# Weight and x splits of an attention kernel moved to GpSimd, and its last numerator groups put in other PSUM banks

## The chip, the cores and the metric

The kernel runs on one core of one Trainium2 chip. The metric is device time in microseconds for one execution, and less is better. A profiled execution gives besides it a span (first to last instruction) and a trace of every engine.

## What is computed

The reference is FAVOR attention followed by two feed-forward layers, all in float32:

```
q_s, k_s = q * scale, k * scale            # q, k, v: (4, 8, 576, 64), omega: (128, 64)
phi(x):  h = x @ omega.T - |x|^2 / 2;  h -= max(h);  exp(h) / sqrt(128)
kv  = phi(k_s).T @ v;   z = sum over tokens of phi(k_s)
x   = (phi(q_s) @ kv) / (phi(q_s) @ z + 1e-6)
h   = x @ w_in;  x = silu(h) @ w_out                       # 2304 x 512, d_ff 2048
out = (silu(x @ w_gate) * (x @ w_val)) @ w_out2            # d_ff 1536
```

## The kernel before, in words

**Three parts in a row.** First attention (to about 136.8 us of the trace), then the up and down products of the first layer, then those of the second. The feed-forward products use Strassen's scheme: seven block products for eight, on sums of blocks. Each operand goes as two parts, `hi` (a copy rounded to a short float32 form, `F32R`) and `lo` (the rest, original minus `hi`), and three matmuls stand for one (hi*hi, hi*lo, lo*hi).

**Attention.** Eight units (two batches of one pair of heads each, 1152 tokens) of nine chunks of 128 tokens, worked on in pairs of chunks: 36 iterations of `two_steps(d)` (L881), and a few more at the end. An iteration issues, for each engine in its own order: on TensorE `proj` of the next pair (L730, 32 matmuls), `kv` of the pair before (L772), perhaps the numerators of one group of three chunks (`num`, L818, 24 matmuls), the four transposes of `q_turn` (L794), and perhaps the transposes back of a group (`turn`, L850). On VectorE two maxima (`soft`, L752), and for a group `divide` (L838: add, reciprocal, multiply) and `take_out` (L856, copy from PSUM). On ScalarE eight exponentials (L754) and the copy `qp` (L800). `proj` has two sets of two PSUM banks (0 to 3); banks 5 to 7 go round among `kv` sums and groups of numerators in the queue `px` (L666).

**Work put between.** Attention leaves TensorE's operands of the next part to be made. `early` (L504) holds two queues: `conv` (three jobs of `w_in`, one of `w_out`) and `x` (the first of three blocks of the attention's own result). At the end of each iteration `feed` (L508) takes from each queue, for each of two steps and each engine, at most the given number of operations, in order, if their inputs were issued at least some steps ago (`made`) and their space was given back two steps ago (`given`). So the order is settled when the program is built, and on the chip each engine works through its list, waiting on semaphores. A conversion job (`conv_job`, L315) decodes the weights, which arrive in 64-bit words, in two halves: `first` on ScalarE (L343), `shift` (L350) and `low` (L357) on VectorE; then four Strassen sums on GpSimd (L376); then, in four parts of 256, 512, 512 and 512 columns, `hi` (L406 on VectorE, L408 on ScalarE) and `lo` (L419, VectorE). The decoded halves lie in three slots (`f_c`), which the last `lo` of a job gives back, and the next jobs' `first` takes them. `x_prep` (L534) makes seven operands of two parts of 384 columns each: `hi` on ScalarE (L571), `lo` on VectorE (L580), and eight differences (L601), here on GpSimd.

**The end of attention.** Unit 7's three groups of numerators are left over. `last_nums` (L989) issues them after the first Strassen product of the up part (L1060), into banks 7, 6 and 5, with their divides; then `mark(5, 6)` (L1034) writes banks 5 and 6. `last_turn` (L1005) turns each group between later products. In the up part a planner with costs (`Op`, `flush`) sets the order of everything else; the store of hidden values (L1086) and the loads of later x blocks (L553) share the one queue of SyncE (SP).

Of the kernel before, what the change touches and what calls it, by code (L numbers as in the profile page):

```python
# [9 lines left out]
F32 = mybir.dt.float32  # L10
# [32 lines left out]
def kernel(  # L43
# [270 lines left out]

    def conv_job(kind, i, dram=None):  # L315
        b = {}
# [84 lines left out]
        def hi(k):  # L401
            def go():
                if ("w", 0) not in b:
                    b["w", 0], b["w", 1] = f_w.take(), f_w.take()
                if k in (1, 2):
                    nc.vector.tensor_copy(dst(0, k), src(k))  # L406
                else:
                    nc.scalar.activation(dst(0, k), src(k), AF.Copy)  # L408

            n = 256 * (parts[k][1] - parts[k][0])  # L410
            eng, c = ("DVE", cost("COPY", n)) if k in (1, 2) else ("ACT", cost("ACT", n))
            return Op(
                eng, c, go, ins=[key(*x) for x in after[k]], outs=[key("hi", k)],
                slots=lambda: None if ("w", 0) in b else (f_w, 2),
            )

        def lo(k):
            def go():
                nc.vector.tensor_sub(dst(1, k), src(k), dst(0, k).bitcast(F32))  # L419
                if k == 3:  # L420
                    done(clk["end"])
                    W[kind, i] = (b["w", 0], b["w", 1])

            n = 256 * (parts[k][1] - parts[k][0])
            outs = [key("lo", k)] + ([("W", kind, i)] if k == 3 else [])
            return Op("DVE", cost("DVE", n), go, ins=[key("hi", k)], outs=outs)

# [80 lines left out]
    def feed(name, s, limits):  # L508


        for e, n in limits.items():
            q = early[name]
            for _ in range(n):
                o = next((o for o in q if o.eng == e), None)
                if o is None or o.ready() is None:
                    break
                if any(k in made and s - made[k][0] < made[k][1] for k in o.ins):
                    break
                slots = o.slots() if callable(o.slots) else o.slots
                if slots is not None and any(s - given.get(id(x), -9) < 2 for x, _ in list(slots[0].q)[: slots[1]]):  # L520
                    break
                q.remove(o)
                now[0] = s
                o.emit()
                for k in o.outs:
                    made[k] = (s, {"SP": 5 if name == "x" else 3, "POOL": 2}.get(e, 1))
        while urgent:
            urgent.pop(0).emit()
# [5 lines left out]
    def x_prep(m, s, raws, temps, eng, early=False, before=None, after=(), then=None):  # L534
# [31 lines left out]
        def hi(name, of, j, after):  # L566
            def go():
                if (m, s, name) not in X:
                    X[m, s, name] = tuple(f_op.take() for _ in range(2))
                o = cut(X[m, s, name][0], j * N, N)  # L570
                nc.scalar.activation(o, (b[of, j] if (of, j) in b else r[of, j]).bitcast(F32), AF.Copy)  # L571

            return Op(
                "ACT", cost("ACT", N), go, ins=[after], outs=[key("hi", name, j)], slots=(f_op, 2) if j == 0 else None
            )

        def lo(name, of, j):
            def go():
                h, l = (cut(x, j * N, N) for x in X[m, s, name])
                nc.vector.tensor_sub(l, (b[of, j] if (of, j) in b else r[of, j]).bitcast(F32), h.bitcast(F32))  # L580
                if name == "T4" and temps:
# [7 lines left out]
            if name == "T4":  # L589
                outs.append(key("end", j))  # L590
            return Op("DVE", cost("DVE", N), go, ins=[key("hi", name, j)], outs=outs)

# [275 lines left out]
    def store(u):  # L868
        B, p = u_of(u, 0)
        for b in range(UB):  # L870
            T["xd", B, p + b] = 0.0
            made["xd", B, p + b] = (step_of[0], 3)
        nc.sync.dma_start(
            out=x_d[B][p : p + UB].rearrange("b p s -> p b s"), in_=xts.pop(u).rearrange("p (b s) -> p b s", b=UB)
        )

    groups, to_divide, to_turn, to_take = [], [], [], []

    early["conv"].extend(chain(conv_job("in", 0), conv_job("in", 1), down_job(0, 0), conv_job("in", 2)))
    early["x"].extend(x_prep(0, 0, xr1, False, "POOL", early=True))  # L880
    def two_steps(d):  # L881
# [28 lines left out]
        coming = sum((u, b) not in kvps and LEFT[u, b] == NCH // 2 + 1 for u, b in {x[:2] for y in kv_parts(d) for x in y}) if 0 <= d < ND else 0  # L910
        if groups and groups[0][2] < d and len(px) and len(px) - 1 + len(turns) + len(ended) >= coming and not (groups[0][:2] != (NU - 1, 0) and groups[0][0] == NU - 1) and d < ND:
            u, g, _ = groups.pop(0)
# [15 lines left out]
        if d < ND:  # L928
# [8 lines left out]
            for s in (2 * d, 2 * d + 1):  # L937
                step_of[0] = s
                if s >= 8:
                    feed("conv", s, {"SP": 1, "ACT": 1, "DVE": 1, "POOL": 1})  # L940
                if s >= 27:
                    feed("x", s, {"SP": 4, "ACT": 2, "DVE": 2, "POOL": 1})

# [45 lines left out]
    def last_nums():  # L989

        for (u, g, _), b in zip(left_over, (7, 6, 5)):
            num(u, g, b)
# [643 lines left out]
```

## Time and profile before

| | before |
|---|---|
| median of 3 runs | 916.19 us (915.04 to 919.54) |
| the profiled execution's own time | 919.76 us |
| its span | 917.6 us |
| TensorE busy, share of the span | 883.3 us, 96% |
| VectorE | 641.3 us, 70% |
| ScalarE | 558.0 us, 61% |
| GpSimd | 120.8 us, 13% |

Engines: PE is TensorE's matmuls, PEld its weight loads, DVE is VectorE, ACT ScalarE, POOL GpSimd, SP SyncE. The ends of matmuls are modelled, so a busy PE is not one at its peak; the pace of PE is better read from the starts of the same step in successive iterations. The shares of the whole span say little about attention, which is a seventh of it.

### The profile page before, as it was taken

The numbers are of one execution on the slowest core, as the hardware profiler recorded it, in microseconds if no ns is written. First come the engines' busy times: TensorE is split into PE (matmuls) and PEld (weight loads), VectorE is DVE, ScalarE is ACT, GpSimd is POOL, SyncE is SP. The second block draws the span as 40 slices with busy tenths as digits, with TensorE's granted clock in tenths as the row PEclk, the third lists the DMA queues.
The fourth block names the chain that finished last, engine by engine and source line by source line (L and its number), as shares of the span: only waits on it lengthen the run. The fifth ranks groups of instructions, "written<-read, shape, count | busy, mean of one in ns | idle before, by whom it ended". The sixth has DMA issues, their size and how long they took to land.

```text
span 917.6 us, 18106 instructions
## 1 busy us (share of the span) xinstructions
PE 883.3 (96%) x6887; PEld 856.2 (93%) x6887; DVE 641.3 (70%) x1048; ACT 558.0 (61%) x1186; POOL 120.8 (13%) x152
## 2 busy tenths in 40 slices
PE   8988899999999998999999999999999999999998
PEld 7777689899999988999998999999999998999997
DVE  3897877665664497686789898574646547959683
ACT  5988787666667774444457775554545357445553
POOL 0112300214344000000000024130303100000000
PEclk9999999999999999999999999999999999999999
DMA  6676507858989984707604746362625168371702
GB/s 208 225 232 213 175 29 253 260 176 287 299 277 366 373 325 120 225 1 216 197 23 157 231 148 215 112 224 70 230 75 188 64 219 297 102 237 53 240 1 70
DMA packets 105864, 170.08 MB, mean 185 GB/s; under 512 B 8752, under 2 KB 87984, under 8 KB 105776
## 3 DMA queue, kind: packets, MB, share of 16 engines
q1 hardware_dynamic: 104608, 168.33, 55.7%
q8 instruction: 54, 0.88, 0.4%
q10 hardware_dynamic: 1168, 0.59, 0.2%
q14 instruction: 34, 0.28, 0.1%
HBM read 107.02 MB, written 61.87 MB: 184 GB/s over the span
## 4 chain that ended last, share of the span: by engine, by line
PE 73%; DVE 12%; ACT 7%; DMA 5%; issue 2%; POOL 0%; SPq 0%; ACTq 0%; DVEq 0%; POOLq 0%
PE ps L1060 38%; PE ps L1427 31%; ACT kq L754 3%; DVE nb L752 2%; DMA fa<-in_moe_w_out 2%; PE ps L738 1%; DVE ra L419 1%; DVE ra L1290 1%; PE ps L798 1%; DVE fa L357 1%; DVE nt L844 1%; PE ps L782 1%; DMA rb<-wd_out 1%; DVE fa L1134 1%; DMA wd_out<-fa 1%
## 5 line engine op out<-in xcount | busy, mean ns | idle before, releaser
L376 POOL TENSOR_TENSOR fa<-fa 128x256 f32<-128x256 f32 x136 | 111.8, 836 | 604.6 <-DVE fa L357 368.9
L1060 PE MATMUL ps<-rb,ra 128*128 128x384 f32 x840 | 158.8, 342 | 2.3 <-ACT ps L1077 2.3
L1060 PE MATMUL ps<-ra 128*128 128x384 f32 x840 | 156.6, 336 | 1.9 <-ACT ps L1077 1.8
L1060 PE MATMUL ps<-rc,ra 128*128 128x384 f32 x840 | 156.1, 338 | 0.1
L1060 PEld LDWEIGHTS ps<-rb,ra 128*128 128x128 f32 x840 | 149.6, 190 | 3.5 <-ACT ps L1077 3.5
L1060 PEld LDWEIGHTS ps<-ra 128*128 128x128 f32 x840 | 146.5, 188 | 3.4 <-ACT ps L1077 3.2
L1060 PEld LDWEIGHTS ps<-rc,ra 128*128 128x128 f32 x840 | 147.7, 188 | 0.8 <-ACT ps L1077 0.8
L1286 ACT ACTIVATE ra<-fa 128x768 fp32r<-128x768 f32 x105 | 87.9, 844 | 80.8 <-PE ps L1427 65.5
L1077 ACT ACTIVATE ps<-ps 128x384 f32<-128x384 f32 x180 | 85.3, 475 | 84.9 <-PE ps L1060 78.6
L1290 DVE TENSOR_TENSOR ra<-fa,ra 128x768 fp32r<-128x768 f32 x105 | 100.5, 957 | 48.9 <-PE ps L1427 31.9
L1134 DVE TENSOR_TENSOR fa<-fa,ps 128x384 f32<-128x384 f32 x120 | 66.2, 551 | 96.8 <-ACT ps L1077 76.2
L1427 PE MATMUL ps<-ra,rb 128*128 128x384 f32 x720 | 128.5, 339 | 0.0
L1427 PEld LDWEIGHTS ps<-ra,rb 128*128 128x128 f32 x720 | 127.1, 188 | 0.4 <-DVE ra L1290 0.3
L1427 PE MATMUL ps<-ra 128*128 128x384 f32 x612 | 108.9, 335 | 6.7 <-DVE ra L1290 6.5
L1427 PEld LDWEIGHTS ps<-ra 128*128 128x128 f32 x612 | 106.0, 188 | 8.8 <-DVE ra L1290 7.9
L754 ACT ACTIVATE kq<-ps,nb 128x128 f32<-128x128 f32 x288 | 80.0, 398 | 15.8 <-DVE nb L752 12.2
L1427 PE MATMUL ps<-ra,rc 128*128 128x384 f32 x432 | 78.2, 340 | 1.5 <-DVE ra L1290 1.4
L1427 PEld LDWEIGHTS ps<-ra,rc 128*128 128x128 f32 x432 | 76.1, 188 | 2.8 <-DVE ra L1290 2.7
L1101 ACT ACTIVATE fa<-fa 128x384 f32<-128x384 f32 x84 | 43.8, 522 | 29.5 <-DVE fa L1134 29.2
L1310 DVE TENSOR_TENSOR fa<-ra,fa 128x768 f32<-128x768 f32 x63 | 60.1, 954 | 0.7
L1286 ACT ACTIVATE ra<-ra 128x768 fp32r<-128x768 f32 x42 | 35.5, 845 | 34.5 <-PE ps L1427 31.9
L1290 DVE TENSOR_TENSOR ra<-ra 128x768 fp32r<-128x768 f32 x42 | 40.2, 958 | 20.9 <-PE ps L1427 9.3
(84 smaller groups left out, 981.7 us busy)
## 6 DMA issues: line engine op xcount, KB each, us to landing
g_d<-fa SPq DMA_DIRECT2D x168, 192.0 KB, 3.5
fa<-g_d SPq DMA_DIRECT2D x42, 384.0 KB, 4.4
ra<-g_d SPq DMA_DIRECT2D x42, 384.0 KB, 4.2
fa<-in_moe_w_out SPq DMA_DIRECT2D x28, 512.0 KB, 5.5
fa<-in_moe_w_in SPq DMA_DIRECT2D x16, 512.0 KB, 4.4
wd_out<-fa SPq DMA_DIRECT2D x14, 512.0 KB, 3.4
fa<-in_moe_w_gate SPq DMA_DIRECT2D x12, 512.0 KB, 4.0
fa<-in_moe_w_val SPq DMA_DIRECT2D x12, 512.0 KB, 5.5
```

The costliest lines, as they stand in the source:

```text
L357: nc.vector.scalar_tensor_tensor(c, word(h, 0), 29, c, op0=ALU.logical_shift_right, op1=ALU.bitwise_or)
L376: f(blk(f"S{n}"), blk(l), blk(r))
L752: nc.vector.reduce_max(nb, x, axis=AX.X, negate=True)
L754: nc.scalar.activation(e[:, g // 2, g % 2, h * M : (h + 1) * M], x[:, g, :], AF.Exp, bias=nb[:, g : g + 1])
L1060: nc.tensor.matmul(ps[b][:, :N], cut(l, j * P, P), cut(r, j * N, N), start=start and c == 0, stop=stop and c == 5, skip_group_check=True,)
L1077: nc.scalar.activation(out() if callable(out) else out, src, AF.Copy)
L1101: nc.scalar.activation(b["t"], src, AF.Silu)
L1134: nc.vector.tensor_add(t, t if in_place else p5[n], ps[bank_][:, :N])
L1286: nc.scalar.activation(ops[s, p, k][0], src(), AF.Copy)
L1290: nc.vector.tensor_sub(l, src(), h.bitcast(F32))
L1310: (nc.gpsimd if eng == "POOL" else nc.vector).tensor_sub(z(PLACE[to]), z(PLACE.get(l, l)), z(PLACE.get(r, r)))
L1427: nc.tensor.matmul(ps[BANKS[p] + e][:, :N], cut(a, e * P, P), b, start=p in FIRST and i == 0 and c == 0, stop=p in LAST and i == fp - 1 an ...
```

## The change

`conv_job(..., side=True)` (the three `w_in` jobs of `early`) and the early `x_prep` issue all of `hi` and `lo` on GpSimd; `hi` becomes a `tensor_scalar` (times 1.0, times 1.0). `feed` allows two GpSimd operations a step, and no distance is wanted between operations of one engine. At d = 35 banks 1 and 0 join `px`, a group of numerators may be issued at d = 36 too, and `last_nums` uses banks 7 and 1 for the two groups that are left.

```diff
-    def conv_job(kind, i, dram=None):
+    def conv_job(kind, i, dram=None, side=False):
...
-                if k in (1, 2):
+                if side:
+                    nc.gpsimd.tensor_scalar(dst(0, k), src(k), 1.0, 1.0, op0=ALU.mult, op1=ALU.mult)
+                elif k in (1, 2):
                     nc.vector.tensor_copy(dst(0, k), src(k))
                 else:
                     nc.scalar.activation(dst(0, k), src(k), AF.Copy)
...
+            if side:
+                eng, c = "POOL", cost("POOL", n)
...
-                nc.vector.tensor_sub(dst(1, k), src(k), dst(0, k).bitcast(F32))
+                (nc.gpsimd if side else nc.vector).tensor_sub(dst(1, k), src(k), dst(0, k).bitcast(F32))
...
-                if any(k in made and s - made[k][0] < made[k][1] for k in o.ins):
+                if any(k in made and made[k][2] != e and s - made[k][0] < made[k][1] for k in o.ins):
...
-                    made[k] = (s, {"SP": 5 if name == "x" else 3, "POOL": 2}.get(e, 1))
+                    made[k] = (s, {"SP": 5 if name == "x" else 3, "POOL": 2}.get(e, 1), e)
...
-                nc.scalar.activation(o, (b[of, j] if (of, j) in b else r[of, j]).bitcast(F32), AF.Copy)
-
+                i = (b[of, j] if (of, j) in b else r[of, j]).bitcast(F32)
+                if early:
+                    nc.gpsimd.tensor_scalar(o, i, 1.0, 1.0, op0=ALU.mult, op1=ALU.mult)
+                else:
+                    nc.scalar.activation(o, i, AF.Copy)
+
+            eng = "POOL" if early else "ACT"
...
-                nc.vector.tensor_sub(l, (b[of, j] if (of, j) in b else r[of, j]).bitcast(F32), h.bitcast(F32))
+                f = nc.gpsimd if early else nc.vector
+                f.tensor_sub(l, (b[of, j] if (of, j) in b else r[of, j]).bitcast(F32), h.bitcast(F32))
...
-    early["conv"].extend(chain(conv_job("in", 0), conv_job("in", 1), down_job(0, 0), conv_job("in", 2)))
+    early["conv"].extend(chain(conv_job("in", 0, side=True), conv_job("in", 1, side=True), down_job(0, 0), conv_job("in", 2, side=True)))
...
+        if d == ND - 1:
+            px.extend((1, 0))
-        if groups and groups[0][2] < d and len(px) and len(px) - 1 + len(turns) + len(ended) >= coming and not (groups[0][:2] != (NU - 1, 0) and groups[0][0] == NU - 1) and d < ND:
+        if groups and groups[0][2] < d and len(px) and len(px) - 1 + len(turns) + len(ended) >= coming and not (groups[0][:2] != (NU - 1, 0) and groups[0][0] == NU - 1) and d <= ND:
...
-                    feed("conv", s, {"SP": 1, "ACT": 1, "DVE": 1, "POOL": 1})
+                    feed("conv", s, {"SP": 1, "ACT": 1, "DVE": 1, "POOL": 2})
                 if s >= 27:
-                    feed("x", s, {"SP": 4, "ACT": 2, "DVE": 2, "POOL": 1})
+                    feed("x", s, {"SP": 4, "ACT": 2, "DVE": 2, "POOL": 2})
...
-        for (u, g, _), b in zip(left_over, (7, 6, 5)):
+        for (u, g, _), b in zip(left_over, {2: (7, 1), 3: (4, 7, 1)}[len(left_over)]):
```

How this moves instructions, in three places. On VectorE, around iterations 8 and 9, before (L752 the maxima, L841 to L844 a divide, L863 a copy out, L406 and L419 the split of the first weight job):

```order
L752 TENSOR_REDUCE nb<-ps_79 128x4
L863 COPY fa<-ps_84 128x384
L406 CAST ra<-fa 128x512
L419 TENSOR_TENSOR ra<-fa,ra 128x256
L752 TENSOR_REDUCE nb<-ps_80 128x4
L841 TENSOR_SCALAR rc<-ps_83 128x6
L842 RECIPROCAL rc<-rc 128x6
L844 TENSOR_TENSOR nt<-ps_83,rc 128x384
L752 TENSOR_REDUCE nb<-ps_81 128x4
L809 COPY st<-ps_85 128x130
L419 TENSOR_TENSOR ra<-fa,ra 128x512
L406 CAST ra<-fa 128x512
```

and in the changed kernel (its lines stand about 12 lower):

```order
L764 TENSOR_REDUCE nb<-ps_79 128x4
L875 COPY fa<-ps_84 128x384
L764 TENSOR_REDUCE nb<-ps_80 128x4
L853 TENSOR_SCALAR rc<-ps_83 128x6
L854 RECIPROCAL rc<-rc 128x6
L856 TENSOR_TENSOR nt<-ps_83,rc 128x384
L764 TENSOR_REDUCE nb<-ps_81 128x4
L821 COPY st<-ps_85 128x130
L350 TENSOR_SCALAR fa<-fa 128x512
```

The splits are gone from between the maxima; the decoding of the next weight job (L350) comes up an iteration earlier.

On GpSimd, where attention had only sums (L376) and eight differences (L601), the first weight job now reads:

```order
L376 TENSOR_TENSOR fa<-fa 128x256 x4
L406 TENSOR_SCALAR ra<-fa 128x256
L406 TENSOR_SCALAR ra<-fa 128x512
L423 TENSOR_TENSOR ra<-fa,ra 128x256
L423 TENSOR_TENSOR ra<-fa,ra 128x512
L406 TENSOR_SCALAR ra<-fa 128x512 x2
L423 TENSOR_TENSOR ra<-fa,ra 128x512 x2
```

A job has 12 instructions there instead of 4, and the x block 36 instead of 8.

On TensorE at the end of attention, before (L782 `kv`, L798 `q_turn`, L854 `turn`, L1037 `mark`, L1060 the first product, L829 `num`; ps_83, 84, 85 are banks 5, 6, 7, and ps_79 is bank 1):

```order
L782 MATMUL ps_85<-v_99,kq 64x65 x8
L798 MATMUL ps_82<-ident,kq 128x128 x4
L854 MATMUL ps_84<-ident,nt 128x128 x3
L1037 MATMUL ps_80<-ra 128x384
L1037 MATMUL ps_81<-ra 128x384
L1060 MATMUL ps_78<-ra 128x384 x6
L829 MATMUL ps_85<-st,qp 64x65 x12
L829 MATMUL ps_84<-st,qp 64x65 x12
L829 MATMUL ps_83<-st,qp 64x65 x12
L1037 MATMUL ps_83<-ra 128x384
L1037 MATMUL ps_84<-ra 128x384
L1060 MATMUL ps_80<-ra 128x384 x6
```

and in the changed kernel:

```order
L794 MATMUL ps_85<-v_99,kq 64x65 x8
L841 MATMUL ps_83<-st,qp 64x65 x12
L810 MATMUL ps_82<-ident,kq 128x128 x4
L866 MATMUL ps_84<-ident,nt 128x128 x3
L866 MATMUL ps_83<-ident,nt 128x128 x3
L1051 MATMUL ps_80<-ra 128x384
L1051 MATMUL ps_81<-ra 128x384
L1074 MATMUL ps_78<-ra 128x384 x6
L841 MATMUL ps_85<-st,qp 64x65 x12
L841 MATMUL ps_79<-st,qp 64x65 x12
L1051 MATMUL ps_83<-ra 128x384
L1051 MATMUL ps_84<-ra 128x384
```

One group and its turn now stand ahead of the first product, and the two groups left no longer write the banks that `mark` writes right behind them. (A row marked x12 is 24 matmuls in two halves of the array.)

## Rows read from the trace of the kernel before

**Rows 1.** Windows: length, busy time by engine (instructions), granted clock, DMA share, GB/s

```profile
14.27:38.01 23.74, 23.66 (x537) 19.82 (x535) 16.98 (x37) 21.65 (x73) 3.15 (x4) 1.00 0.56 191
38.01:120.35 82.34, 70.66 (x1516) 59.00 (x1514) 70.08 (x151) 68.46 (x217) 17.33 (x20) 0.96 0.59 195
120.35:135.83 15.48, 15.04 (x342) 12.76 (x338) 12.02 (x27) 14.40 (x48) 0.00 (x0) 1.00 0.11 41
```

**Rows 2.** Timeline of PE (start, us, what), the transposes of three late iterations

```profile
125.85 0.66 PE L798 MATMUL ps<-ident,kq 128*128 128x128 f32 x4
...
129.37 0.66 PE L798 MATMUL ps<-ident,kq 128*128 128x128 f32 x4
...
131.66 0.66 PE L798 MATMUL ps<-ident,kq 128*128 128x128 f32 x4
```

**Rows 3.** Groups of DVE, 38.01 to 120.35: busy us, mean ns | idle before

```profile
L844 DVE TENSOR_TENSOR nt<-ps,rc 128x384 f32<-128x384 f32 x15 | 8.4, 557 | 0.5
L419 DVE TENSOR_TENSOR ra<-fa,ra 128x512 fp32r<-128x512 f32 x9 | 7.0, 773 | 1.8 <-ACT ra L408 1.8
L357 DVE SCALAR_TENSOR_TENSOR fa<-fa 128x512 uint32<-128x512 uint32 x6 | 4.1, 688 | 0.1
L580 DVE TENSOR_TENSOR ra<-xr,ra 128x384 fp32r<-128x384 f32 x6 | 4.1, 681 | 0.0
...
L580 DVE TENSOR_TENSOR ra<-fa,ra 128x384 fp32r<-128x384 f32 x6 | 3.7, 621 | 5.5 <-ACT ra L571 5.5
...
L350 DVE TENSOR_SCALAR fa<-fa 128x512 uint32<-128x512 uint32 x6 | 2.5, 419 | 2.7 <-ACT fa L343 2.7
...
L406 DVE CAST ra<-fa 128x512 fp32r<-128x512 f32 x5 | 2.1, 419 | 0.0
L419 DVE TENSOR_TENSOR ra<-fa,ra 128x256 fp32r<-128x256 f32 x2 | 2.1, 1034 | 0.0
```

**Rows 4.** Groups of ACT in the same stretch

```profile
L571 ACT ACTIVATE ra<-fa 128x384 fp32r<-128x384 f32 x7 | 3.8, 550 | 0.0
L571 ACT ACTIVATE ra<-xr 128x384 fp32r<-128x384 f32 x6 | 3.3, 550 | 0.0
L408 ACT ACTIVATE ra<-fa 128x512 fp32r<-128x512 f32 x3 | 2.0, 668 | 0.0
L408 ACT ACTIVATE ra<-fa 128x256 fp32r<-128x256 f32 x2 | 0.9, 449 | 0.0
```

**Rows 5.** Windows behind two pauses of PE inside attention

```profile
77.00:80.00 3.00, 3.00 (x39) 2.67 (x39) 2.60 (x7) 2.12 (x7) 0.00 (x0) 0.53 1.04 383
...
111.00:115.00 4.00, 4.00 (x59) 3.55 (x63) 2.89 (x7) 3.11 (x11) 0.00 (x0) 0.57 0.40 151
```

**Rows 6.** Groups of POOL, 38.01 to 120.35

```profile
L376 POOL TENSOR_TENSOR fa<-fa 128x256 f32<-128x256 f32 x12 | 9.1, 765 | 46.5 <-DVE fa L357 29.7 <-DVE xt L863 12.9 <-ACT kq L754 3.8
...
L601 POOL TENSOR_TENSOR fa<-fa 128x384 f32<-128x384 f32 x4 | 4.0, 1006 | 7.6 <-DVE ra L580 7.6
```

**Rows 7.** Groups of POOL in the whole span

```profile
masks.py:199 POOL TENSOR_SCALAR_AFFINE_SELECT ident<-ident 128x128 f32<-128x128 f32 x1 | 0.3, 293 | 0.1
```

**Rows 8.** Timelines of DVE and POOL: splits and differences that meet, and one that does not

```profile
106.59 1.33 POOL L601 TENSOR_TENSOR xr<-xr 128x384 f32<-128x384 f32 x1
...
106.98 1.35 DVE L580 TENSOR_TENSOR ra<-xr,ra 128x384 fp32r<-128x384 f32 x1
...
148.12 0.55 DVE L601 TENSOR_TENSOR fa<-fa 128x384 f32<-128x384 f32 x1
```

**Rows 9.** Timeline of PE, from the end of attention into the up products

```profile
135.83 0.66 PE L798 MATMUL ps<-ident,kq 128*128 128x128 f32 x4 [0.41 <-ACT qp L800]
...
138.15 2.32 PE L829 MATMUL ps<-st,qp 128*64 128x65 f32 x72
141.94 0.62 PE L1037 MATMUL ps<-ra 128*128 128x384 f32 x2 [1.46 <-DVE nt L844]
...
178.11 10.17 PE L1060 MATMUL ps<-rb,ra 128*128 128x384 f32 x48 [2.08 <-ACT ps L1077]
```

More of the change, by code (lines that the diff above doesn't have):

```diff
@@ L425, in lo @@
             outs = [key("lo", k)] + ([("W", kind, i)] if k == 3 else [])
-            return Op("DVE", cost("DVE", n), go, ins=[key("hi", k)], outs=outs)
+            eng = "POOL" if side else "DVE"
+            return Op(eng, cost(eng, n), go, ins=[key("hi", k)], outs=outs)
         def store(a, z, src, ins):
@@ L570, in go @@
                 o = cut(X[m, s, name][0], j * N, N)
-                nc.scalar.activation(o, (b[of, j] if (of, j) in b else r[of, j]).bitcast(F32), AF.Copy)
+                i = (b[of, j] if (of, j) in b else r[of, j]).bitcast(F32)
[4 more added lines that the diff above has]
+            eng = "POOL" if early else "ACT"
             return Op(
-                "ACT", cost("ACT", N), go, ins=[after], outs=[key("hi", name, j)], slots=(f_op, 2) if j == 0 else None
+                eng, cost(eng, N), go, ins=[after], outs=[key("hi", name, j)], slots=(f_op, 2) if j == 0 else None
             )
@@ L590, in lo @@
                 outs.append(key("end", j))
-            return Op("DVE", cost("DVE", N), go, ins=[key("hi", name, j)], outs=outs)
+            eng = "POOL" if early else "DVE"
+            return Op(eng, cost(eng, N), go, ins=[key("hi", name, j)], outs=outs)
         def sub(to, l, rr, j, ins, out, temp=None):
@@ L871, in store @@
             T["xd", B, p + b] = 0.0
-            made["xd", B, p + b] = (step_of[0], 3)
+            made["xd", B, p + b] = (step_of[0], 3, "out")
         nc.sync.dma_start(
```

## The prediction

> **What bounds the kernel now.** I read the windows first, cut at the transposes of three iterations of attention: 8 iterations from 14.27 us, 21 from 38.01, 6 from 120.35 [rows 1]. In the middle stretch the splits of weights and x run; in the other two there are few or none. The 21 iterations take 82.34 us, 3.92 each; the 8 ahead of them take 2.97 each and the 6 behind 2.58. So it is this stretch that has something to give. In it no engine is full: PE is busy 70.66 us, DVE 70.08, ACT 68.46. They hand each iteration round (projection on PE, maximum on DVE, exponentials on ACT, products on PE again), and a split that stands in DVE's list between two maxima holds all three up. In the last 6 iterations, with DVE busy 12.02 of 15.48 us, PE is busy 15.04: freed of splits, PE sets the pace.
>
> What pace that is I read from starts on PE's timeline [rows 2]. From 129.37 to 131.66 an iteration without numerators takes 2.29 us; the one before took 3.52, with a group. So a group of numerators with its turn costs 3.52 - 2.29 = 1.23 us. The stretch holds 15 groups, by the divides in it [rows 3]. PE alone would need 21 x 2.29 + 15 x 1.23 = 66.5 us for it. Twice in the stretch PE also ran at about half clock, 0.53 and 0.57 granted in the windows behind pauses (between the levels 1.2 and 2.4 GHz) [rows 5]; a stretch without such pauses would be spared that, and the 66.5 us, read at full clock, has it in already.
>
> **The change part by part.** *Taken off DVE.* In the stretch: nine wide and two narrow `lo` of weights, 7.0 + 2.1 us, twelve `lo` of x, 4.1 + 3.7, five `hi` of weights, 2.1 [rows 3]: 19.0 us of groups. From 70.1 that leaves about 51. *Taken off ACT*: thirteen `hi` of x, 3.8 + 3.3, and five of weights, 2.0 + 0.9 [rows 4]: 10.0 us, leaving about 58.5 of 68.5. Both then lie under PE's 66.5, so PE is what is late next.
>
> *Put on POOL.* For three weight jobs and the x block, by the code: two-input instructions, 16 sums and 3 narrow `lo` of 256 columns, 9 `lo` of 512, and 8 differences and 14 `lo` of 384. Of these the rows have 765 ns for 256 columns and 1006 for 384 [rows 6], so 1.88 ns a column, and an estimate of 1.25 us for 512. Sum: 19 x 0.765 + 9 x 1.25 + 22 x 1.006 = 47.9 us. Then 26 `hi`, one input each, for which no row of the kernel has the operation: 3 of 256, 9 of 512, 14 of 384 columns. The nearest rows are the mask's one-input select, 293 ns for 128 columns [rows 7], and the two-input price. By the columns of the select and no fixed part it would be 1.17 us for 512, and with a fixed part less; I take the two-input price, 2.3 + 11.3 + 14.1 = 27.6 us, as it is the dearer and the better measured. Together 75.5 us. POOL may start with the first decoded half, near 28 us as now, and its last operand, T4, is first used by the eighth product of the up part: seven products of six matmuls, at most 1.27 us each by 48 matmuls in 10.17 us, and 2.32 us of numerators [rows 9], make 11 us behind attention's end. Attention will end near 124 us by the sum below, so there are 107 us for 75.5, and POOL's own time is covered. If that cover were gone, the wait would come earlier: ScalarE's `first` on the second half of job 1 needs a slot that the last `lo` of job 0 gives back. In the program's order four iterations lie between (some 13.5 us at 3.4), and the eleven POOL instructions in them take about 11.3 us. Behind that `first` in ACT's list stand the exponentials, so a late POOL stops everything; here it has about 2 us to spare. SP is touched once: the store of the `w_out` sums waits for POOL's sums, which now stand behind x splits; loads behind it are for later iterations.
>
> *What POOL does to DVE.* Of DVE's work the decoding stays, `shift` and `low`, six of each in the stretch [rows 3]. The trace shows what a meeting costs: POOL's difference at 106.59 and DVE's `lo` at 106.98 took 1.33 and 1.35 us, where a like instruction of DVE takes 0.55 alone [rows 8], so 0.8 us more. If none of the 12 meets POOL, the stretch falls to 66.5 us; if each waits 0.8 and all of it shows, to 66.5 + 9.6 = 76.1. POOL will be at work in most of that time but DVE has some 15 us to spare, so I take the middle, 71.3: a gain of 11.0 us. The Trainium skill has a rule that speaks against this change: "SBUF — State Buffer", section "Who interferes with whom", lets GpSimd hold the port pair that it shares with VectorE for a whole instruction, while the other blocks fully; "Perfetto Trace Analysis", section "Optimizing Scalar/DVE Operations", adds that moving work between the two might therefore not help. The row above agrees as to the meeting; how often it happens decides, and that is the first rival.
>
> For the price of `hi` the page "GPSIMD Engine Reference", section "Engine selection", calls one-input work roughly line-rate; at its 1.2 GHz that is an estimate of 0.43 us for 512 columns and 9 us for all 26 without fixed parts, and POOL's sum would be 57 us. No row here shows it.
>
> *The end of attention.* The numerators of one group, a third of 2.32 us, move to where PE now waits 0.41 us for ACT, and the pause of 1.46 us before `mark` goes, since the divides no longer hold banks 5 and 6 [rows 9]. PE's work stays the same. Added is a wait: the moved group's turn stands on PE ahead of the first product and needs its divide, about 1 us with its last step of 0.56 [rows 3], of which the four transposes, 0.66 us, and another turn cover most. At best 1.9 us are gained, at worst 1.0; I take 1.4. Next to be late would be the divide of the first remaining group, at its turn, but a product lies between.
>
> *Behind it.* In the up part the planner shuffles weight conversions and loads a little. PE there waits once, 2.08 us at 178.11 [rows 9], and ran at half clock behind it; this may go or come again, so 3 us each way, middle 0. Everything later starts when it starts.
>
> Sum: 11.0 + 1.4 = 12.4 us. The profiled execution's own 919.76 us would be 907.4; the median of the runs lies 3.57 lower, at 916.19, so the forecast against it is 903.8.
>
> **The rivals.** *The port eats the gain.* If POOL's instructions stand back to back and each of the 12 decodings waits out a whole one of 1.25 us on the path, the stretch takes 66.5 + 15.0 = 81.5 us, a gain of 0.8, and with the end's 1.4 the time is 914.0. For it: POOL will have two operations a step and DVE's decoding always finds company. Against: the one clean meeting cost 0.8, and DVE has spare time now. This is what the rule of the Trainium skill would make of it. Chance 0.12.
>
> *POOL becomes the bound, and the kernel is slower.* The unknown is `hi`. Let it cost k times the two-input price. Job 0's instructions then take 6.8 + 4.5k us against 13.5, and both jobs' slots stop ACT; the last operand is ready at 28 + 47.9 + 27.6k. At k = 3 ACT waits twice 6.8 us, T4 comes at 159 where 148.6 is wanted, and 13.6 + 10 - 12.4 gives 11 us more: 927. It turns at about k = 2.6, a `hi` of 512 columns in 3.3 us. For it: no row shows the operation, and two multiplications are asked of it. Against: the select's row. Chance 0.08.
>
> *PE's floor is reached.* No meeting costs anything, the stretch takes 66.5 us, the end gives 1.9 and the pause at 178 goes with its half clock: 15.8 + 1.9 + 3 = 20.7 us less, 895.5. For it: the last 6 iterations are that good now. Against: three engines within a few us of each other rarely fit so well, and six `first` stay on ACT. Chance 0.12.
>
> **How the numbers follow.** My forecast has the other 0.68: a gain of 12.4 us, on its own terms from 4 (6.2 in the stretch, 1.0 at the end, 3 lost behind) to 20, so 896 to 912. The range for eight in ten leaves out the slower rival and the outer part of the floor: 897 to 914, where the port's case just fits. A measurement can tell 0.5%, 4.6 us, from no change. The forecast and the floor are faster by more, but for some 0.02 of the forecast's lower edge, and a little of the port's case comes with them: 0.80. The port's case and that edge make no change: 0.12. Slower: 0.08.
>
> **What would show it.** In the changed profile the iterations between the 9th and the 30th transposes should come every 3.2 to 3.6 us, DVE should be busy some 55 us in them, POOL some 65, and the half-clock windows inside attention should be gone. `shift` and `low` should show up to 0.8 us more each. POOL's `hi` of 512 columns should take at most 1.25 us, and ACT should never wait for a `lo` on POOL. Before `mark` the pause should be gone, and a shorter one stand before the moved turn. It is wrong if exponentials wait on POOL, if DVE's decoding takes the place of its splits on the chain, or if the up part's first products wait for x operands.

## The result, and the profile after

The changed kernel takes 901.65 us (median, 900.87 to 902.58) where the kernel before, run beside it, takes 915.62 us (914.79 to 919.54). The ratio is 0.984, with an interval from 0.9809 to 0.987: 14 us faster. The forecast was 903.8 us, in a range of 897 to 914.

Its profiled execution has 901.76 us, 0.1 off its median. That of before had 919.76, which lies 4 us above its median here; so the two traces differ by more (17.55 us of span) than the medians do. On the three other chips that ran the kernel before, its medians were 918.69, 920.11 and 919.44; on the last of them the changed kernel ran again and had 902.44, a gain of 17.0 (ratio 0.9818, 0.9792 to 0.9844). The gain is 14 to 17 us. The first chip's median of before rests on four executions (914.79 to 919.54), where the others gave 914.9 to 922.93; whether that chip differs is not shown.

The head of the changed kernel's profile: span, and busy time by engine.

```profile
span 900.0 us, 18108 instructions
...
PE 876.9 (97%) x6887; PEld 853.0 (95%) x6887; DVE 628.9 (70%) x1016; ACT 548.4 (61%) x1166; POOL 161.4 (18%) x204
```

GpSimd has 40.6 us more than the 120.8 of before, VectorE 12.4 less, ScalarE 9.6 less. What that does to the time these totals don't say. The windows do, cut at the transposes of the same iterations (columns as in [rows 1]):

```profile
14.53:38.23 23.70, 23.62 (x536) 19.77 (x534) 15.86 (x34) 21.58 (x74) 5.84 (x9) 1.00 0.56 192
38.23:106.78 68.55, 65.07 (x1517) 55.66 (x1513) 56.03 (x124) 59.22 (x197) 46.70 (x58) 1.00 0.71 234
106.78:122.46 15.68, 15.66 (x366) 13.46 (x362) 10.87 (x25) 13.95 (x48) 8.43 (x10) 1.00 0.11 41
```

Against [rows 1] the first and the last stretch are as long as before. The 21 iterations between them fell from 82.34 to 68.55 us: 13.8 of the 17.55. In them VectorE's busy time fell by 14.1 us and ScalarE's by 9.2, GpSimd's rose by 29.4, and the granted clock went from 0.96 to 1.00: the two half-clock windows of [rows 5] are gone. PE is busy 65.07 of 68.55 us. It is now the engine that the others wait for. For the same matmuls its busy time fell by 5.6 us, which goes with the clock, and its idle time by 8.2, from 11.7 to 3.5. What PE waited for in the stretch (from, to, total, times, longest), the two largest before and then the largest after:

```profile
PE ps L829 <- DVE fa L863: 5.4, 3, 2.5
PE ps L738 <- ACT kq L754: 3.4, 6, 0.9
```

```profile
PE ps L841 <- DVE fa L875: 2.6, 2, 1.4
```

The numerators' wait for VectorE's copy out of PSUM was halved, and the projections' wait for exponentials fell from 3.4 to 0.5 us.

The end of attention, on PE's timeline (start, us, what):

```profile
123.62 0.55 PE L866 MATMUL ps<-ident,nt 128*128 128x128 f32 x3 [0.17 <-DVE nt L856]
...
125.50 1.62 PE L841 MATMUL ps<-st,qp 128*64 128x65 f32 x48
127.05 0.62 PE L1051 MATMUL ps<-ra 128*128 128x384 f32 x2
...
140.49 8.59 PE L1074 MATMUL ps<-ra 128*128 128x384 f32 x48 [1.75 <-ACT ps L1091]
```

Where 72 numerators stood behind attention and `mark` waited 1.46 us for a divide [rows 9], 48 stand now and `mark` follows with no wait. The moved group's turn waits 0.17 us for its divide. From the last transposes to this `mark` it is 127.05 - 122.46 = 4.59 us, before 141.94 - 135.83 = 6.11: 1.5 us less. But in the up part a new pause of 1.75 us stands at 140.49: PE waits for ScalarE's copies out of PSUM (L1091). ScalarE itself had been waiting for weights, whose load SP had issued at 132.54 (timelines of ACT and of SP):

```profile
138.99 0.66 ACT L343 ACTIVATE fa<-fa 128x512 f32<-128x512 f32 x1 [1.43 <-DMA fa<-in_moe_w_in]
```

```profile
132.54 0.41 SPq L322 DMA_DIRECT2D fa<-in_moe_w_in  x1
```

The planner put `first` of the next weight job into ScalarE's list where it thought the weights had landed, and they had not. On the other side the old pause of 2.08 us at 178.11 [rows 9] is gone. From this `mark` to the first product of the down part it is 184.06 us, before 185.91: 1.85 less. All behind it takes 588.9, before 589.7; in the other traces of this case that part takes 588.5 to 590.6, with nothing changed in it, so these 0.8 us are within its scatter.

The decoding that VectorE kept (groups of DVE, 38.23 to 106.78), and GpSimd's groups up to 130 us:

```profile
L357 DVE SCALAR_TENSOR_TENSOR fa<-fa 128x512 uint32<-128x512 uint32 x6 | 4.7, 786 | 0.1
L350 DVE TENSOR_SCALAR fa<-fa 128x512 uint32<-128x512 uint32 x6 | 3.2, 532 | 2.7 <-ACT fa L343 2.7
```

```profile
L376 POOL TENSOR_TENSOR fa<-fa 128x256 f32<-128x256 f32 x16 | 11.7, 743 | 51.8 <-DVE fa L357 42.1 <-DMA wd_out<-fa 9.4
...
L423 POOL TENSOR_TENSOR ra<-fa,ra 128x512 fp32r<-128x512 f32 x9 | 11.6, 1296 | 0.0
...
L591 POOL TENSOR_TENSOR ra<-fa,ra 128x384 fp32r<-128x384 f32 x7 | 7.0, 1000 | 0.5
...
L406 POOL TENSOR_SCALAR ra<-fa 128x512 fp32r<-128x512 f32 x9 | 5.5, 615 | 0.0
...
L578 POOL TENSOR_SCALAR ra<-fa 128x384 fp32r<-128x384 f32 x7 | 3.6, 512 | 0.4
```

`low` went from 688 to 786 ns and `shift` from 419 to 532 [rows 3]: over six each, 1.3 us. On GpSimd the two-input instructions cost what the prediction took (1.296 us for 512 columns, estimate 1.25). The one-input `hi` costs 0.615 us, half of the 1.25 taken.

### The profile page after: what moved, and what is told of

The parts are those of the page before. It is cut to its first block, busy times and chain, and to the rows that moved or that the text cites. A ratio compares the mean times of both kernels' runs of the same rounds, so it can differ in the third digit from the quotient of the medians.

```text
span 900.0 us, 18108 instructions
## 1 busy us (share of the span) xinstructions
PE 876.9 (97%) x6887; PEld 853.0 (95%) x6887; DVE 628.9 (70%) x1016; ACT 548.4 (61%) x1166; POOL 161.4 (18%) x204
## 4 chain that ended last, share of the span: by engine, by line
PE 85%; DVE 5%; ACT 4%; DMA 3%; issue 2%; SPq 0%; DVEq 0%; ACTq 0%
PE ps L1074 45%; PE ps L1441 31%; PE ps L750 3%; PE ps L794 2%; PE ps L810 2%; ACT kq L766 2%; PE ps L841 1%; DMA rawq<-in_q 1%; DVE ra L1304 1%; DMA fa<-in_moe_w_in 1%; DMA fa<-in_moe_w_out 1%; DVE rc L1256 1%; DVE ra L423 1%; DMA ra<-wu_val 1%; DMA om<-in_omega 0%
## 5 line engine op out<-in xcount | busy, mean ns | idle before, releaser
L376 POOL TENSOR_TENSOR fa<-fa 128x256 f32<-128x256 f32 x136 | 111.4, 832 | 554.4 <-DVE fa L357 322.1
L1091 ACT ACTIVATE ps<-ps 128x384 f32<-128x384 f32 x180 | 85.5, 476 | 86.3 <-PE ps L1074 80.1
L764 DVE TENSOR_REDUCE nb<-ps 128x4 f32<-128x512 f32 x72 | 47.8, 683 | 10.0 <-PE ps L750 5.1
```

The source lines that it names most:

```text
L376: f(blk(f"S{n}"), blk(l), blk(r))
L764: nc.vector.reduce_max(nb, x, axis=AX.X, negate=True)
L1091: nc.scalar.activation(out() if callable(out) else out, src, AF.Copy)
```

## The experiments

Each kernel was compared with the kernel before, run beside it on the same chip. "The stretch" is the time of the same 21 iterations. The kernels with `hi` three and six times, with `lo` twice, and the second trace of before have one execution each.

### The kernel before, profiled once more

No edit. The question was whether the prediction's base, one profiled execution that stood above its median, was an accident.

> The kernel before, profiled a second time, to see how much of the 17.6 us between the two spans is the one execution. The medians differ by 14.0 us only. Theory: the three half-clock windows and the pause at 178 us differ from execution to execution, and this span lies near 914 us, with the 21 iterations at 79 to 82 us. Rival: the span is near 917.6 again and the medians' difference is what varies.

Measured: 919.78 us for the profiled execution, span 917.6 again, where its median on this chip was 918.69. The stretch:

```profile
38.29:120.74 82.45, 70.65 (x1517) 58.99 (x1514) 70.08 (x151) 68.36 (x217) 17.33 (x20) 0.96 0.60 195
```

It repeats [rows 1] to 0.1 us, pauses and clock included, so the rival's first half holds: the trace of before was no accident. (With the end alone changed, below, the stretch takes 82.63.) The stretch of before thus repeats to 0.3 us; that of the changed kernel, as the next traces show, does not.

### The change at the end alone

The kernel before, with only the last groups' banks and place changed:

```diff
+        if d == ND - 1:
+            px.extend((1, 0))
...
-        for (u, g, _), b in zip(left_over, (7, 6, 5)):
+        for (u, g, _), b in zip(left_over, {2: (7, 1), 3: (4, 7, 1)}[len(left_over)]):
```

(and `d <= ND` for the groups.)

> Before, with the last groups of numerators alone changed (banks 7 and 1, one group at d = 36); all splits where they were. Theory: the pause of 1.46 us before mark goes and the stretch of 21 iterations stays near 82 us, so 1.0 to 1.9 us less: about 914.1. Rival (the end of attention holds back the loads and products behind it too): 3 to 4 us less, about 912.

Measured: 915.92 us against 918.69 (ratio 0.997, 0.9949 to 0.9991): 2.8 us less, between the two expectations. The stretch takes 82.63, unchanged, and the span of the profiled execution is 916.5 us, 1.1 under before. PE's timeline shows the wait at the moved turn and a pause in the up part:

```profile
137.70 0.55 PE L854 MATMUL ps<-ident,nt 128*128 128x128 f32 x3 [0.17 <-DVE nt L844]
...
154.59 10.17 PE L1062 MATMUL ps<-ra 128*128 128x384 f32 x48 [1.77 <-ACT ps L1079]
```

The pause before `mark` is gone, the turn waits 0.17 us as in the changed kernel, and the up part has one pause, of 1.77 us, as before and the changed kernel have. The end is worth its 1 to 2 us with or without the splits moved. The rest of the 2.8 lies within the interval (0.8 to 4.7 us).

### The splits alone

The changed kernel with the end as before (the lines above taken back).

> The changed kernel with the last groups as before (banks 7, 6, 5, none at d = 36). Theory: the stretch of 21 iterations takes 68 to 69 us as in the changed kernel, the pause before mark is back, 903.2 us. Rival (the parts need each other): above 906.

Measured: 903.49 us against 918.69 (ratio 0.9821, 0.9789 to 0.9853). So nearly all of the gain comes from the splits. But the profiled stretch takes 72.70 us, 4 more than the 68 to 69 expected, though the program of this stretch is the same, instruction for instruction:

```profile
36.56:109.26 72.70, 67.85 (x1517) 58.05 (x1514) 57.66 (x124) 59.30 (x197) 46.65 (x58) 0.95 0.67 221
```

The difference is in the first two iterations of the stretch, which take 6.71 + 5.40 us, and in the changed kernel 4.87 + 3.27: 4.0 us. DVE and POOL, PE's longest wait (from, to, total, times, longest), and the window behind it, first in the kernel with the splits alone:

```profile
37.56 1.61 DVE L350 TENSOR_SCALAR fa<-fa 128x512 uint32<-128x512 uint32 x1 [1.29 <-ACT fa L343]
```

```profile
37.61 2.67 POOL L423 TENSOR_TENSOR ra<-fa,ra 128x512 fp32r<-128x512 f32 x2
```

```profile
PE ps L841 <- DVE fa L875: 2.6, 1, 2.6
```

```profile
42.00:47.00 5.00, 5.00 (x65) 4.22 (x65) 2.98 (x7) 3.00 (x12) 0.73 (x1) 0.50 0.67 225
```

and the same place of the changed kernel:

```profile
39.23 0.43 DVE L350 TENSOR_SCALAR fa<-fa 128x512 uint32<-128x512 uint32 x1 [1.28 <-ACT fa L343]
```

```profile
39.29 2.71 POOL L423 TENSOR_TENSOR ra<-fa,ra 128x512 fp32r<-128x512 f32 x2
```

```profile
42.26 0.92 PE L841 MATMUL ps<-st,qp 128*64 128x65 f32 x24 [1.39 <-DVE fa L875]
```

In both, `shift` and a `lo` on GpSimd start 50 to 60 ns apart. In the one `shift` takes 0.43 us, in the other 1.61: 1.2 more, about one whole `lo` (1.3 us). That lateness stands in VectorE's list ahead of a copy out of PSUM (L875), on which the next numerators wait, so PE stands still for 2.6 us, where in the changed kernel it waits 1.39 us at the same place and its clock stays at 1.00. Behind the longer pause it runs at half clock (0.50 granted, so 1.2 GHz, from 42 to 47 us). One meeting so costs 4 us, and a difference of some 10 ns in two starts goes with it; that it decides which of the two waits is not shown.

Other traces agree. By the length of this one `shift`, the two iterations take 8.1 us (0.43 us, in the changed kernel, in three more traces of its attention and with `hi` three times), 8.6 (0.61 us, with shorter instructions), 10.4 (1.38 us, with `lo` twice) and 12.1 (1.61 us, here). It may be what spreads the times of this kernel: its four executions took 899.81, 903.12, 903.86 and 906.4 us at mean granted clocks of 1.000, 0.998, 0.996 and 0.994, though only the last has a trace, and in other kernels time and clock do not always go together.

So the stretch of the changed program is not one number. Five traces have it: 68.55 in the changed kernel and 70.00 in its second trace, 69.30 and 68.37 in the two with another landing time (which leaves attention as it is), and 72.70 here. The 1.45 us of the second trace lie elsewhere, in its iterations 8 to 10:

```profile
36.28:106.28 70.00, 65.25 (x1518) 55.77 (x1514) 56.13 (x124) 59.38 (x197) 46.32 (x58) 1.00 0.71 229
```

Against 82.34 to 82.63 in three traces with the splits in place, the gain is 9.6 to 14.3 us.

### `lo` alone, and `hi` alone

The changed kernel with `hi` left on ScalarE and VectorE (`lo` alone moved):

```diff
-                if side:
+                if False:
                     nc.gpsimd.tensor_scalar(dst(0, k), src(k), 1.0, 1.0, op0=ALU.mult, op1=ALU.mult)
```

> The changed kernel with hi left where it was (ScalarE, and VectorE's two casts a job); only lo on GpSimd. VectorE is freed of 17 us in the stretch, ScalarE of nothing and stays at about 68 us of work, above TensorE's 66.5. Theory (all three engines hand the iteration round, so ScalarE's hi between exponentials holds it up): the stretch takes 72 to 76 us, 905 to 909 us. Rival (VectorE alone was the bound): 68 to 69 us, 901.7 us.

and with `lo` left on VectorE (`hi` alone moved); in both, the x block likewise:

```diff
-                (nc.gpsimd if side else nc.vector).tensor_sub(dst(1, k), src(k), dst(0, k).bitcast(F32))
+                nc.vector.tensor_sub(dst(1, k), src(k), dst(0, k).bitcast(F32))
```

> The changed kernel with lo left on VectorE; only hi on GpSimd. In the stretch ScalarE is freed of its 10 us, VectorE of 2.1 us of casts only, and its 17 us of two-input lo now meet GpSimd more often. Theory (the gain is VectorE's): the stretch takes 77 to 82 us, the time is 1 to 5 us under before. Rival (ScalarE's list is as good a relief): 70 to 73 us, as with lo alone.

Measured: `lo` alone 904.67 us against 918.69 (ratio 0.9846, 0.9825 to 0.9868), `hi` alone 910.18 against 920.11 (0.9903, 0.9873 to 0.9933). The stretches, `lo` alone and then `hi` alone:

```profile
37.99:109.00 71.01, 66.04 (x1517) 56.27 (x1513) 57.16 (x129) 64.82 (x211) 33.48 (x35) 1.00 0.69 226
```

```profile
37.37:114.00 76.63, 67.73 (x1516) 57.69 (x1513) 69.44 (x148) 60.66 (x197) 30.47 (x42) 0.98 0.64 209
```

By these single traces `lo` alone gives 11.3 of the 13.8 us, `hi` alone 5.7; together they give less than their sum (17.0), as they must if PE's pace, 66.5 us, is a floor under both. The expectation that `hi` hardly counts is wrong: with VectorE still busy 69.44 us, the relief of ScalarE by some 8 us is worth 5.7 in the stretch, and by the medians `hi` alone is 9.9 us under before, where 1 to 5 were expected. `lo` alone came out below its theory's 72 to 76, above its rival's 68 to 69, and 0.3 us under its 905. Since the changed program's own stretch varies from 68.4 to 72.7, what `hi` adds to `lo` is not shown by one trace each; by the medians on one chip (904.67 with `lo` alone and the end changed, 903.49 with both and the end as before) it would be 1 to 3 us, within their scatter.

### `hi` dearer: the slower rival made

Every `hi` on GpSimd issued six times, and in a second kernel three times, x block and weights alike; the shorter form is written again with the same values.

```diff
-                    nc.gpsimd.tensor_scalar(dst(0, k), src(k), 1.0, 1.0, op0=ALU.mult, op1=ALU.mult)
+                    for _ in range(6):
+                        nc.gpsimd.tensor_scalar(dst(0, k), src(k), 1.0, 1.0, op0=ALU.mult, op1=ALU.mult)
```

> The changed kernel with each hi on GpSimd issued six times: same values, six times the time. Measured, a hi of 512 columns takes 0.62 us, so six take 3.7, three times the two-input price, the case of the prediction's slower rival. Theory (GpSimd late stops ScalarE at the next job's decode and TensorE at the last x operands): about 11 us slower than before, and ScalarE's decode waits some 7 us for GpSimd's lo, twice. Rival (nobody waits for GpSimd): as the changed kernel.

Measured, six times: 949.16 us against 920.11. The `hi` took 86.9 us in all, 3.1 times the price that the prediction took, which is the slower rival at k = 3. The stretch, what ScalarE waited for in attention, and what PE waited for up to 200 us:

```profile
37.24:126.24 89.00, 70.98 (x1517) 59.92 (x1514) 57.05 (x124) 59.77 (x197) 81.81 (x125) 0.90 0.56 180
```

```profile
ACT fa L343 <- POOL fa L376: 4.8, 1, 4.8
...
ACT fa L343 <- POOL ra L424: 3.8, 1, 3.8
```

```profile
PE ps L1076 <- POOL ra L580: 13.9, 3, 5.6
```

Two parts of the mechanism are as the rival had them: ScalarE's `first` waits for GpSimd with the exponentials behind it (8.6 us), and the up part's products wait for x operands (13.9 us, the rival's term was 10). The size is not: 29 us slower, where it gave 11. The stretch grew by 20.4 us for 8.6 us of waits of ScalarE. The four iterations with these waits take 11.2 us more than in the changed kernel, with PE at 0.50 from 89.5 to 96 us. A fifth takes 8.5 more (11.92 for 3.46), and in it PE waits for loads. PE's longest wait there, and the longest of SP's queue:

```profile
PE ps L752 <- DMA rawq<-in_q: 5.6, 1, 5.6
```

```profile
SPq L441 <- POOL fa L376: 18.2, 1, 18.2
```

The store of the `w_out` sums stood 18.2 us in SP's queue until GpSimd had made them, and the loads of x, q and k behind it went out in a bunch: `rawq` was issued 1.9 us ahead of that iteration, in the changed kernel 5.2. The prediction names this queue and puts it at nothing ("loads behind it are for later iterations"); here it is the largest single loss in the stretch.

> The changed kernel with each hi on GpSimd issued three times: 29 us more of one-input work there, 91 us in all, about 1.5 times the two-input price for a hi, under the 2.6 at which the prediction's slower rival turns. Theory (until GpSimd is late at ScalarE's decode nobody waits for it; job 0 then takes about 13.7 us against some 13.3): the stretch 68 to 71 us, the time within 2 us of the changed kernel. Rival (each us on GpSimd counts): 10 us or more above the changed kernel.

Measured, three times: 905.82 us against 919.44, and the stretch takes 68.56 us, as in the changed kernel:

```profile
38.16:106.72 68.56, 65.06 (x1517) 55.64 (x1513) 57.00 (x124) 59.26 (x197) 60.82 (x85) 1.00 0.72 234
```

So 29.6 us more on GpSimd, 14.1 of them in the stretch, cost attention nothing: its cover is real. The total is 3.4 us above the changed kernel's median on the same chip (902.44, of 901.38 to 905.0), outside the expected 2. The two profiled spans differ by 3.7: the part ahead of the stretch is 1.9 longer, the stretch 1.4 shorter, and the rest behind the up part 1.1 longer, all within what traces of one program differ by. From the second `mark` to the first down product it is 186.74 for 184.62 us, 2.1 more, and there the pause, 1.92 on the same chip, is 3.41:

```profile
142.50 3.67 PE L1076 MATMUL ps<-ra 128*128 128x384 f32 x12 [3.41 <-ACT ps L1093]
```

The queue of SP shows why it grew (124 to 136 us):

```profile
SPq L559 <- POOL xr L615: 3.5, 1, 3.5
```

A load of a later x block waits 3.5 us for GpSimd's last differences, and the weights' load behind it is issued at 134.92, in the first trace of the changed kernel at 132.54. ScalarE then waits 1.94 us for these weights, not 1.43, and PE 3.41. So GpSimd's added work cost time outside attention, by SP's queue.

### The port: more two-input work

Every `lo` on GpSimd issued twice: nearly the same extra time for GpSimd as `hi` three times, but in two-input instructions.

```diff
-                (nc.gpsimd if side else nc.vector).tensor_sub(dst(1, k), src(k), dst(0, k).bitcast(F32))
+                for _ in range(2 if side else 1):
+                    (nc.gpsimd if side else nc.vector).tensor_sub(dst(1, k), src(k), dst(0, k).bitcast(F32))
```

> The changed kernel with each lo on GpSimd issued twice: 28 us more of two-input work there, as much time as in hi_x3, but in instructions of 1.3 us that read two tensors. Theory (only meetings with VectorE's 12 decodings cost, up to 1.3 us each, and few meet): 1 to 3 us above hi_x3. Rival (what counts is GpSimd's time alone): as hi_x3 within 1 us.

Measured: 903.71 us against 919.44, 2.1 under `hi` three times, where 1 to 3 above was expected. The stretch takes 71.10, 2.5 more than there:

```profile
37.08:108.18 71.10, 66.44 (x1517) 56.90 (x1514) 58.55 (x124) 59.17 (x197) 61.55 (x69) 0.98 0.70 226
```

VectorE's decoding with `hi` three times, and with `lo` twice:

```profile
L357 DVE SCALAR_TENSOR_TENSOR fa<-fa 128x512 uint32<-128x512 uint32 x6 | 5.9, 984 | 0.1
...
L350 DVE TENSOR_SCALAR fa<-fa 128x512 uint32<-128x512 uint32 x6 | 3.2, 526 | 2.7 <-ACT fa L343 2.7
```

```profile
L357 DVE SCALAR_TENSOR_TENSOR fa<-fa 128x512 uint32<-128x512 uint32 x6 | 6.9, 1158 | 0.1
...
L350 DVE TENSOR_SCALAR fa<-fa 128x512 uint32<-128x512 uint32 x6 | 3.5, 579 | 2.2 <-ACT fa L343 2.2
```

In all: 6.6 us before [rows 3], 7.9 in the changed kernel, 9.1 with `hi` three times, 10.4 with `lo` twice. With `hi` six times it is 9.3, where GpSimd is busy 81.81 of 89 us: beside the short one-input instructions a `shift` or `low` takes some 0.3 us more, beside a `lo` up to 1.2. So the rival's lock exists, and a meeting with two-input work is the dearer one. But the sum of meetings does not set the stretch. With `hi` three times the 1.2 us more show nowhere in it. With `lo` twice 2.3 of the 2.5 us stand in the first two iterations, behind the same `shift` as in the kernel with the splits alone:

```profile
38.06 1.38 DVE L350 TENSOR_SCALAR fa<-fa 128x512 uint32<-128x512 uint32 x1 [1.27 <-ACT fa L343]
```

And 71.10 lies within the 68.4 to 72.7 of the unchanged program. So this pair of kernels doesn't decide between theory and rival. The total is lower than the other's since the pause in the up part is 2.06 us here and not 3.41.

### Shorter instructions on GpSimd

If a meeting costs the rest of GpSimd's instruction, halves should cost less. The weights' `hi` and `lo` of 512 columns as two of 256 (`hi` likewise):

```diff
+                w = 256 if side else 256 * (parts[k][1] - parts[k][0])
+                for o in range(0, 256 * (parts[k][1] - parts[k][0]), w):
+                    (nc.gpsimd if side else nc.vector).tensor_sub(cut(dst(1, k), o, w), cut(src(k), o, w), cut(dst(0, k), o, w).bitcast(F32))
```

> The changed kernel with each 512-column hi and lo of a weight job on GpSimd as two of 256. GpSimd holds the shared port for at most 0.73 us at a time instead of 1.3. Theory (one meeting of VectorE's shift with a long lo costs up to 1.2 us there and, when TensorE then pauses and its clock halves, 4 us in all; which of the two comes first is a tie that falls either way): the worst shift falls from 1.61 us to 1.2 at most, no execution lies above 903 us where before is 916, the median is the changed kernel's or 1 us less. Rival (meetings do not matter): the same as the changed kernel, with the same scatter.

Measured: 903.25 us against 920.11 (ratio 0.9836, 0.9788 to 0.9883), the stretch 68.88: no gain. The longest `shift` took 0.87 us, but `low` has 1008 ns in the mean, 786 in the changed kernel: cheaper meetings, and more of them. One of its four executions took 905.66 us, where none above 903 was expected, and the scatter (901.92 to 905.66) is like that of the changed kernel on another chip (901.38 to 905.0), as the rival had it. Whether halves would save the kernel from the 4 us of one unlucky meeting isn't shown, since none fell so here.

### A truer landing time

The new pause in the up part came from a load that landed later than the planner thought. So the planner is told that the weights of `w_in` job 3 land 4 us later:

```diff
+                if kind == "in" and i == 3:
+                    T[key("r", h)] = end + 4.0
```

> The changed kernel with the planner told that the fourth w_in job's raw weights land 4 us later, so that ScalarE's decode of them stands later in its list than the copies that TensorE needs. Theory (TensorE's pause of 1.75 us at 140.49 is ScalarE waiting 1.43 us for these weights): the pause goes, 1.5 to 2 us less than the changed kernel, a ratio to before of 0.982. Rival: another wait takes its place, no change from 0.984.

Measured: 900.69 us against 920.11 (ratio 0.9808, 0.977 to 0.9845). ScalarE's `first` moved from 138.99 to 147.98 us, and the pause was gone. It was then run beside the changed kernel on one chip.

> The changed kernel again, beside the next one on the same chip: a ratio to before near 0.984, and the pause of about 1.75 us near 140 us in its profile.

> late_first again, beside the changed kernel. Theory (the pause near 140 us was worth its own length): 1.0 to 2.0 us under the changed kernel, 0.1 to 0.2% more off. Rival: the earlier difference was the chip's, within 0.5 us.

Measured: the changed kernel 902.44 us (ratio 0.9818, 0.9792 to 0.9844), with the landing time 899.08 (0.978, 0.9752 to 0.9807). PE in the changed kernel, and with the landing time:

```profile
140.17 6.01 PE L1074 MATMUL ps<-ra 128*128 128x384 f32 x33 [1.92 <-ACT ps L1091]
```

```profile
130.94 16.00 PE L1076 MATMUL ps<-ra 128*128 128x384 f32 x90
```

The pause of 1.92 us is gone. From the second `mark` to the first down product it takes 183.01 us (126.78 to 309.79), in the changed kernel 184.62 (126.56 to 311.18): 1.6 us less, within the 1 to 2 expected; on the earlier chips it was 182.17 for 184.06. Behind it the part with no change takes 1.4 us more, and both profiled executions have a span of 900.3 us. The medians differ by 3.4, but the two intervals overlap. So 1.6 us are shown up to the down part, and a gain of the whole is not shown beyond the medians, by which this is the fastest version.

## Why the prediction was right, by its steps

**What bounds the kernel: right.** The windows had put the gain into the 21 iterations with splits, and there it was. PE's pace read from three starts, 66.5 us for the stretch, was its floor: it came within 2.1 us of it. In five traces of the same program it came within 1.9 to 6.2. What is left in the first is little: PE waits for a copy out of PSUM (L875) for 2.6 us in all, ahead of numerators.

**What VectorE and ScalarE lose: right.** VectorE was forecast busy some 55 us in the stretch (56.03), ScalarE 58.5 (59.22). With `lo` alone and `hi` alone each part proved to count by itself.

**What meetings cost: the mis-sized term.** The prediction took the middle, 4.8 us, of a range from nothing to 12 x 0.8. VectorE's decoding grew by 1.3 us, and the stretch gained 13.8 where 11.0 was said; only five of the twelve met anything in the profiled execution. The form of the term was wrong too: it adds up twelve meetings, and the runs show that their sum hardly counts, but that one of them, the first `shift`, costs up to 4 us, since a copy that PE needs stands behind it and PE then runs at half clock. Over the five traces the stretch lies 1.9 to 6.2 us above the floor, 3.3 in the mean, so 4.8 was near the size without the mechanism, which is luck. The rival in which the port eats the gain is excluded: 72.70 us at worst, and 71.10 with every `lo` doubled, against its 81.5.

**GpSimd's price: two-input right, `hi` too dear.** 47.9 us were forecast for the two-input instructions, and they cost that. `hi` cost 14.5 us and not 27.6, so GpSimd was busy 62.4 us for 75.5, and in the stretch 46.7 where some 65 were named as the sign. In time it changed nothing, as that work is covered: in attention no wait of ScalarE on GpSimd is in the trace, and `hi` three times cost the stretch nothing, though 2.1 us behind it. The slower rival needs `hi` at 2.6 times the price taken; it had 0.53. At 3.1 it was indeed slower, by the two waits named and by a third that the prediction had put at nothing: loads behind a store in SP's queue. That step was wrong; at the real price of `hi` PE waited 0.4 us for such loads in the whole stretch, so the forecast did not suffer from it.

**The end of attention: right.** 1.4 us were forecast and 1.5 came, with the wait of 0.17 us before the moved turn, and none before `mark`. **Behind it** 1.85 + 0.8 us were gained, inside the 3 allowed, by the chance that was named: one pause went and another came. The 0.8 is within the scatter of that part.

**The sum.** Stretch 13.8, end 1.5, behind 2.7, less 0.4 in the first and last iterations: 17.55 us of span, where 12.4 was forecast. Against the medians of the first chip 14.0 show. The forecast of 903.8 came 2.2 us too high because the meetings cost less than taken and the pause at 178 went; the base (the trace's time set against the median) took 3.5 us of that back. So the closeness of the total is in part luck: by the two profiled executions 18.0 us were gained, 5.6 more than forecast, and the span's 17.55 us lie nearer to the 20.7 of the rival in which PE's floor is reached.

Not tried: the decoding taken off VectorE altogether, which would show a stretch without any meeting; the wider allowance of `feed` by itself, which every kernel with moved splits has too; and why the kernel before has a median 3 to 4.5 us lower on the first chip.

## What to carry to other kernels

Where three engines hand an iteration round and none is full, look for work of no hurry that stands in one engine's list between two steps of the chain: moving it to an idle engine paid here although each piece is slower there, as long as neither the slots it gives back nor a transfer queue that waits for its results is on the chain. Price the cover by making the moved work three and six times as dear, not by busy shares, and follow every queue that waits for it: a store that waits holds up the loads behind it. Take several traces of the same program before reading differences of a few us in a stretch; here the same instructions took 68.4 to 72.7. When the list changes, look anew at every place where a planner guessed a landing time, for a wait in front of an engine's list stops all that is behind it.

## What the runs showed of the hardware that was not expected

A one-input `tensor_scalar` with two multiplications, float32 to the short form, took 512 ns for 384 columns and 615 for 512 on GpSimd, about half of the two-input subtraction of the same width (1000 and 1296). Two instructions of VectorE and GpSimd that started 50 to 60 ns apart went either way: 0.43 us in one kernel and 1.61 in another for the same `shift`. Beside a row of one-input GpSimd instructions of 0.5 to 0.6 us the meetings were cheaper: `low` took 0.98 us for 0.68 alone. And such a delay of 1.2 us cost 4 us, as TensorE's pause behind it brought it down to half clock for the iteration that followed.
